# Decode of two layers on one core: both batches' values in one accumulator half, and three of eight value parts weighted on VectorE

## The chip, the cores and the metric

The kernel runs on 1 core of one Trainium2 chip. The metric is device time in microseconds (us), the median of several executions. Engines: PE (TensorE; PEld is its weight load), DVE (VectorE), ACT (ScalarE), POOL (GpSimd), SP (SyncE), whose queue issues nearly all the transfers here. A line such as L738 is a line of the kernel before.

## The reference

Two rounds of the same pair of blocks, on one new token of each of two batches: attention against a cache of 8192 keys and values, then a gated MLP. All in 32-bit floats.

```python
def _A_ref(x, k_cache, v_cache, wq, wo):          # x: 2 x 1 x 576, caches: 2 x 32 x 8192 x 128
    q = (x @ wq).reshape(2, 1, 32, 128).transpose(0, 2, 1, 3)
    scores = jnp.einsum("bhqd,bhkd->bhqk", q, k_cache) * (128 ** -0.5)
    p = _softmax(scores, axis=-1)
    o = jnp.einsum("bhqk,bhkd->bhqd", p, v_cache)
    return o.transpose(0, 2, 1, 3).reshape(2, 1, 32 * 128) @ wo

def _B_ref(x, w_gate, w_up, w_down):              # 576 -> 4608 -> 576
    return (_gelu(x @ w_gate) * (x @ w_up)) @ w_down

x = x + _A_ref(_layernorm(x), k_cache, v_cache, wq, wo)
x = x + _B_ref(_layernorm(x), w_gate, w_up, w_down)
x = x + _A_ref(_layernorm(x), k_cache, v_cache, wq, wo)
x = x + _B_ref(_layernorm(x), w_gate, w_up, w_down)
```

The caches are 268 MB each and both are read once in each round.

## The kernel before

**Items.** One round's attention is cut into 34 items. Items 0 to 29 are pairs: two neighbouring heads of one batch, 128 partitions by 128 rows of 128 floats, so 8.39 MB of keys and as much of values; batches alternate, so items 2k and 2k + 1 are the same two heads of batch 0 and of batch 1. Items 30 to 33 are single heads. The first layer goes through them from 0 to 33, the second from 33 to 0; a few keys and values at the turn are kept on the chip. An item has 8 parts (4 for a single head) of 16 rows each.

**Space.** `space` is one tile of SBUF in six slots; a pair of slots holds the keys or the values of one item, so three such buffers exist. `Arena` and `queue` plan the transfers when the program is built: a load is written into SP's queue as soon as the buffer it needs has been released by the code so far. In the steady part the values of item n go into the buffer that the keys of item n leave (released by the last reduction, L770), and the keys of a later item into the buffer that the values of item n leave (released by the matmul of the fold, L878). SP issues them in this order, keys and values in turn, and each waits for the instructions that release its buffer.

**Keys.** `multiply` (L738, DVE) multiplies keys with the query, which lies in PSUM (`bank`), in three units of 48, 48 and 32 rows; POOL adds the two halves of each row (L767); DVE adds up the 64 that are left (L770). `peak` and `highest` (L794 to L804) find the greatest score by way of a transpose on PE, `softmax` (L819, L827, ACT) writes the exponentials into `prz`, `total` and `inverse` (L835, L841) give the factor.

**Values.** `prz` holds the exponentials of an item with gaps of zeros, so that 8 neighbouring columns are the weights of a matmul: 4 rows of each of 2 heads. `values` (L899) runs one matmul for 4 rows of values, 128 x 512, into a band of 8 partitions of `acc`; the 4 groups of a part go to 4 bands. The pairs in the middle, 3 to 26, don't do this for all parts: `folds(n)` is true for them, and the last `FOLD` = 2 of 8 parts are weighted on DVE instead. `weigh` adds the exponentials of both heads into `share` (L865; one of them is zero), multiplies the values with them in place (L870), and lets POOL add halves onto each other until 4 rows are left (L873). `folded` (L878) brings these into `acc` by one more matmul, whose weights `owner` say which half of the partitions belongs to which head.

**Out of the accumulator.** `acc` has two halves of 512, and the pairs take them in turn. `gather` takes each item's own entries out of the bands: a product with `diag` (L913) and a sum (L914), on DVE. `context` turns the result by four matmuls (L921) into `po`, and `divide` (L940 on ACT) brings it into `oT`, from where `project` multiplies it with `wo`.

**Order.** The order on each engine is the order of the code, written out by hand (`tc.manual_schedule()`), one pass of the loop per item. In the pass of item n, with p the item before and a the one before that: `weigh(a)` comes first on DVE, ahead of the item's products; on POOL the adds of the fold stand ahead of the item's first L767; `softmax(p)` follows the first product; behind the second product come `total(p)`, `folded(a)`, `gather(a)`, `context(a)` and `values(p)`. Every engine takes its instructions in order.

```python
            if a is not None and folds(a):
                weigh(a)
            for j, (k, m) in enumerate(us):
                multiply(n, k, m)
```

Of the kernel before, what the change touches and what calls it, by code (L numbers as in the profile page):

```python
# [16 lines left out]
B = 2  # L17
# [28 lines left out]
FOLD = 2  # L46
# [78 lines left out]
def decode_layers(ctx, tc, x_in, kc, vc, wq, wo, wg, wu, wd, out):  # L125
# [32 lines left out]
    def part_at(at, n):  # L158
        return space[:, at:at + n]
# [285 lines left out]
    unit = consts.tile([P, 1], F32, name="unit")  # L445
    nc.vector.memset(unit, 1.0)
    ones = unit.to_broadcast([P, P])
    mhalf = consts.tile([P, 1], F32, name="mhalf")
    nc.vector.memset(mhalf, -0.5)

    pick = consts.tile([P, 4], F32, name="pick")
# [4 lines left out]
    diag = consts.tile([P, 4], F32, name="diag")  # L456
    of = consts.tile([P, B], F32, name="of")
    both = ident.rearrange("p (c v b r) -> p b r v c", c=4, v=4, b=B)[:, :, :, 0, :]
    scores = consts.tile([P, 2 * P], F32, name="scores")
    eight = scores[:, 0:4 * B].rearrange("p (b r) -> p b r", b=B)  # L460
    nc.vector.reduce_sum(eight, both, axis=AX.X)
    nc.vector.tensor_add(diag, eight[:, 0, :], eight[:, 1, :])
    nc.vector.reduce_sum(of, eight, axis=AX.X)
# [5 lines left out]
    sums = consts.tile([P, 2, 2], F32, name="sums")  # L469
    nc.vector.memset(sums, 0.0)  # L470

    side = consts.tile([P, 2], F32, name="side")
    nc.vector.reduce_sum(side, pick.rearrange("p (s b) -> p s b", s=2), axis=AX.X)

    owner = consts.tile([P, 2, 4], F32, name="owner")
    nc.vector.memset(owner, 0.0)
    for i in range(2):
        nc.vector.memset(owner[i * HALF:(i + 1) * HALF, i, :], 1.0)

    strip = consts.tile([P, 4], F32, name="strip")  # L480
# [11 lines left out]
    home = consts.tile([P, 3 * DH + 16], F32, name="home")  # L492
# [8 lines left out]
    for s in range(2):  # L501
# [8 lines left out]
    po = bank2[:, 0:2 * GH].rearrange("p (i c) -> p i c", c=2)  # L510
    turned = bank2[:, 2 * GH:2 * GH + P]
    smalls = [bank2[:, 2 * GH + P + 2 * i:2 * GH + P + 2 * i + 2] for i in range(2)]
    low = bank2[:, 2 * GH + P + 8:]
# [5 lines left out]
    rim, cut = two.shape[1] - 2 * DH, mid.shape[1]  # L519
    stash = [  # L520
        (2, rim, DH, low[:, :DH - rim], True),
        (3, 0, DH, low[:, DH - rim:2 * DH - rim], True),
        (4, 0, DH - rim, low[:, 2 * DH - rim:], True), (4, DH - rim, DH, two[:, 2 * DH:], False),
        (5, 0, cut, mid, True), (5, cut, DH, home[:, 3 * DH:], False),
# [77 lines left out]
    def attention(layer):  # L602
# [104 lines left out]
        def multiply(n, k, m):  # L707
# [7 lines left out]
            if n == SINGLE[1] and k == 0 and layer == 0:  # L715
                rest = ready[key_of(n)][2].rearrange("p j d -> p (j d)")[:, (JC - SPLIT[2]) * DH:]
                for to, lo in (
                    (spare, 0), (low, 2 * DH + rim), (qs[:, 2 * DH:], 5 * DH - rim), (mid, 5 * DH),
                    (home[:, 3 * DH:], 5 * DH + cut), (scores[:, DH // 2:DH // 2 + DH], 6 * DH),
# [473 lines left out]
```

## Time and profile before

| | before |
|---|---|
| time, median of 3 | 2683.82 us (2683.8 to 2685.11) |
| the profiled execution | 2683.47 us, span 2681.7 us |
| TensorE clock granted, mean | 0.629 |
| read from HBM | 1152.39 MB, 430 GB/s over the span |
| busy: PE, DVE, ACT, POOL | 912.3, 2027.3, 166.9, 1551.8 us |
| L738, products with the query (DVE) | 223, 1111.8 us |
| L767, adds of half rows (POOL) | 221, 1127.8 us |
| L770, reductions (DVE) | 223, 569.3 us |
| L899, matmuls on values (PE, two records each) | 3328, 509.6 us |
| L870, weighting of values (DVE) | 48, 212.2 us |
| L873, adds of the fold (POOL) | 144, 390.0 us |
| L913 and L914, gather (DVE) | 64 each, 43.5 and 44.2 us |

The span is from the first to the last instruction; the time also holds what lies around it. A row of the timeline has the start in us, the duration, engine, line, operation, what is written and read, shape and count, and in brackets how long the engine stood idle before and what ended that. A row of the groups has count, busy us and mean ns of one, then idle time before and its releasers. SPq is SP's queue: its rows are the issue of a transfer, not the transfer.

### The profile page before, as it was taken

What the parts mean: (1) busy time and instruction counts of PE and PEld (TensorE: products, weight loads), DVE (VectorE), ACT (ScalarE), POOL (GpSimd) and SP (SyncE); (2) the same over time, 40 slices, a digit from 0 to 9 for tenths busy, and PEclk for the clock granted to TensorE, in tenths of its full rate; (3) what the DMA queues carried; (4) which work ended last, traced back from release to release, by engine and by line L of the source; (5) the groups of instructions that cost most, each with busy time, mean ns of one, the idle gap of its engine ahead of it and who ended that gap; (6) DMA issues with size and microseconds to landing.
All of it is one profiled execution on the core that took longest, in us unless ns stands there. A gap on an engine that the chain in (4) does not pass through costs nothing. (4 is left out here: it accounts for less than half of the span.)

```text
span 2681.7 us, 16126 instructions
## 1 busy us (share of the span) xinstructions
PE 912.3 (34%) x6484; PEld 288.9 (11%) x6484; DVE 2027.3 (76%) x979; ACT 166.9 (6%) x797; POOL 1551.8 (58%) x408
## 2 busy tenths in 40 slices
PE   1323332233233233334663333223323323332346
PEld 0100010010001000111221101001000100010012
DVE  4878888888888888867037878888888888888740
ACT  0000000000000000000026000000000000000000
POOL 2546676667666766744028457666766666676520
PEclk8656655665566566566986665566566556655678
DMA  9999999999999999999999999999999999999998
GB/s 422 437 434 428 435 434 433 431 433 433 434 432 434 430 436 434 428 431 427 417 414 426 436 434 429 434 435 434 431 431 435 432 433 434 433 430 436 430 426 382
DMA packets 31498, 1153.44 MB, mean 430 GB/s; under 512 B 3880, under 2 KB 3904, under 8 KB 5696
## 3 DMA queue, kind: packets, MB, share of 16 engines
q1 hardware_dynamic: 31384, 1152.40, 99.8%
q8 instruction: 51, 0.84, 0.1%
q14 instruction: 23, 0.19, 0.0%
q10 hardware_dynamic: 40, 0.01, 0.0%
HBM read 1152.39 MB, written 0.00 MB: 430 GB/s over the span
## 5 line engine op out<-in xcount | busy, mean ns | idle before, releaser
L767 POOL TENSOR_TENSOR space<-space 128x3072 f32<-128x3072 f32 (+4 forms) x221 | 1127.8, 5103 | 474.8 <-DVE space L738 335.1
L738 DVE TENSOR_TENSOR space<-space,bank 128x6144 f32<-128x6144 f32 (+4 forms) x223 | 1111.8, 4987 | 300.4 <-DMA space<-in_A_k_cache_dram 230.6
L770 DVE TENSOR_REDUCE scores<-space 128x48 f32<-128x3072 f32 (+4 forms) x223 | 569.3, 2553 | 91.9 <-POOL space L767 91.7
L873 POOL TENSOR_TENSOR space<-space 128x2048 f32<-128x2048 f32 x144 | 390.0, 2708 | 385.7 <-DVE space L870 362.3
L899 PE MATMUL acc<-space,prz 128*8 128x512 f32 x3328 | 509.6, 776 | 206.6 <-DMA space<-in_A_v_cache_dram 202.5
L653 PE MATMUL bank<-qsb,pick 4*64 4x128 f32 (+1 forms) x256 | 45.4, 432 | 850.9 <-DVE space L738 843.3
L870 DVE TENSOR_TENSOR space<-space,bank 128x4096 f32<-128x4096 f32 x48 | 212.2, 4420 | 1.6
L899 PEld LDWEIGHTS acc<-space,prz 128*8 128x8 f32 x3328 | 98.7, 107 | 559.4 <-issue 356.8
L819 ACT ACTIVATE nbs<-bank 128x2 f32<-128x2 f32 (+1 forms) x68 | 11.6, 171 | 1812.4 <-PE bank L804 1782.8
L921 PE MATMUL bank<-of,wide 128*32 128x2 f32 x512 | 40.9, 202 | 237.9 <-DVE wide L914 237.9
L653 PEld LDWEIGHTS bank<-qsb,pick 4*64 4x64 f32 (+1 forms) x256 | 20.3, 200 | 872.3 <-DVE space L738 855.5
L796 PE MATMUL bank<-ident,m 128*1 128x128 f32 x68 | 21.7, 319 | 242.5 <-DVE m L794 242.3
L575 POOL TENSOR_TENSOR rstd<-ve,mhalf 128x1 f32<-128x1 f32 x4 | 2.2, 550 | 176.0 <-DVE ve L573 176.0
L878 PE MATMUL acc<-space,owner 128*8 128x512 f32 x96 | 89.9, 1039 | 0.0
L1124 DVE STREAM_TRANSPOSE gu<-acc 128x288 f32<-128x288 f32 x4 | 1.9, 483 | 93.2 <-ACT acc L1122 93.2
L921 PEld LDWEIGHTS bank<-of,wide 128*32 128x32 f32 x512 | 35.7, 154 | 326.1 <-DVE wide L914 324.9
L835 PE MATMUL bank<-sums,unit 128*128 128x2 f32 x120 | 35.2, 363 | 86.9 <-ACT prz L827 86.9
L913 DVE TENSOR_TENSOR acc<-acc,diag 128x512 f32<-128x512 f32 x64 | 43.5, 679 | 27.6 <-PE acc L899 27.6
L940 ACT ACTIVATE oT<-bank,rinv 32x8 f32<-32x8 f32 x110 | 28.5, 259 | 381.5 <-PE bank L921 380.8
L827 ACT ACTIVATE prz<-scores,nbs 64x128 f32<-64x128 f32 (+1 forms) x128 | 50.7, 396 | 17.2 <-POOL prz L817 14.4
L760 ACT ACTIVATE space<-space 128x128 f32<-128x128 f32 x164 | 48.4, 296 | 19.4 <-DVE space L738 16.5
L804 PE MATMUL bank<-m,unit 1*128 1x2 f32 (+1 forms) x136 | 38.5, 350 | 25.6 <-DVE m L802 25.6
(100 smaller groups left out, 519.0 us busy)
## 6 DMA issues: line engine op xcount, KB each, us to landing
space<-in_A_k_cache_dram SPq DMA_DIRECT2D x6, 4096.0 KB
space<-in_A_v_cache_dram SPq DMA_DIRECT2D x5, 4096.0 KB
space<-in_A_wo_dram SPq DMA_DIRECT2D x15, 1152.0 KB
space<-in_B_w_gate_dram SPq DMA_DIRECT2D x16, 576.0 KB
space<-in_B_w_up_dram SPq DMA_DIRECT2D x16, 576.0 KB
space<-in_B_w_down_dram SPq DMA_DIRECT2D x8, 1152.0 KB
space<-in_A_v_cache_dram SPq DMA_DIRECT2D x4, 2048.0 KB
space<-in_A_wq_dram SPq DMA_DIRECT2D x16, 512.0 KB
```

What stands on the lines that cost most here:

```text
L653: nc.tensor.matmul(qb[n][to, :], pick[32 * c:32 * c + 4, r:r + 1].to_broadcast([4, P // it.heads]), qsb[32 * c:32 * c + 4, (h % 4) * DH:(h ...
L738: nc.vector.tensor_tensor(out=u[:, :r, :], in0=t[:, :r, :], in1=qb[n].unsqueeze(1).to_broadcast([P, r, DH]), op=ALU.mult)
L760: nc.scalar.activation(u[:, j, :], u[:, j, :], AF.Copy, accum_out=S[n][:, base(n, k) + j:base(n, k) + j + 1])
L767: nc.gpsimd.tensor_tensor(out=half, in0=half, in1=u[:, :r, DH // 2:], op=ALU.add)
L770: nc.vector.tensor_reduce(out=S[n][:, base(n, k):base(n, k) + own_rows(n, k, m)], in_=prod.pop((n, k)), axis=AX.X, op=ALU.add)
L827: nc.scalar.activation(pr[at, lo:].rearrange("p (g e) -> p g e", e=4)[:, 0:it.rows // 2:2, :], s[at, :it.rows].rearrange("p (g r) -> p g r ...
L870: nc.vector.tensor_tensor(out=t, in0=t, in1=share.unsqueeze(2).to_broadcast([P, rows, DH]), op=ALU.mult)
L873: nc.gpsimd.tensor_tensor(out=t[:, :rows], in0=t[:, :rows], in1=t[:, rows:2 * rows], op=ALU.add)
L878: nc.tensor.matmul(accumulator(n)[0:8, :], owner.rearrange("p a e -> p (a e)"), part_at(arena.live[key, lo][0], 4 * DH), start=False, stop ...
L899: nc.tensor.matmul(accumulator(n)[32 * c:32 * c + 8, :], pr[:, at:at + 8], t[g // 4][:, g % 4 * 4:g % 4 * 4 + 4, :].rearrange("p j d -> p ...
L913: nc.vector.tensor_tensor(out=q, in0=q, in1=diag.unsqueeze(2).to_broadcast([P, 4, DH]), op=ALU.mult)
L921: nc.tensor.matmul(po[lo:lo + 32, i, :], t[:, i::GH], of, start=True, stop=True)
```

## The change

Three things are changed together.

1. The two items of the same heads share a half of `acc`. The bands get 16 partitions, 8 for each batch; a matmul on values has 16 columns of weights of which one batch's 8 are zeros. `prz` is one buffer for all pairs, with wider gaps. An item of batch 0 (in the first layer) begins a sum and the item of batch 1 completes it, so `gather`, `context` and `divide` are called once for two items, and `context` and `divide` write four columns instead of two. The constants (`diag`, `of`, `owner` and others) are laid out for this and moved into one tile, `few`.
2. `FOLD` is 3: three of eight parts are weighted and folded, five go to PE by `values`. The fold no longer halves alone: 48 rows become 24, 12, 8 and 4.
3. What was stored in `low` between the layers has less room there; a bit of it goes to a longer `home` (one more copy and one more product).

`weigh(f)` and `folded(f)` are called for every folded item, in the places where they were.

```diff
-FOLD = 2
+FOLD = 3
...
-    po = bank2[:, 0:2 * GH].rearrange("p (i c) -> p i c", c=2)
+    po = bank2[:, 0:4 * GH].rearrange("p (i c) -> p i c", c=4)
...
             if ITEMS[n].heads == 2:
-                return prz[:, 2 * (n % 2):2 * (n % 2) + 2, :].rearrange("p a e -> p (a e)")
+                return prz.rearrange("p a e -> p (a e)")
             return prz[:, n - PAIRS, :]
...
         def accumulator(n):
-            return acc[:, n % 2 if n < PAIRS else (n - PAIRS) // B, :]
+            return acc[:, (n // B + 1) % 2 if n < PAIRS else (n - PAIRS) // B, :]
 
         def completes(i):
 
-            return seq[i] < PAIRS or i > 0 and ITEMS[seq[i - 1]].h == ITEMS[seq[i]].h
+            return i > 0 and ITEMS[seq[i - 1]].h == ITEMS[seq[i]].h
...
             lo = ITEMS[n].parts - FOLD
-            pr = weights_of(n)[:, 2 * JC * lo:2 * JC * (lo + FOLD)].rearrange("p (g a e) -> p a g e", a=2, e=4)
+            pr = weights_of(n)[:, 8 + 4 * JC * lo:8 + 4 * JC * (lo + FOLD)].rearrange("p (g a e) -> p a g e", a=4, e=4)
...
             while rows > 4:
-                rows //= 2
-                nc.gpsimd.tensor_tensor(out=t[:, :rows], in0=t[:, :rows], in1=t[:, rows:2 * rows], op=ALU.add)
+                less = rows // 2 if rows % 8 == 0 else rows - 4
+                nc.gpsimd.tensor_tensor(
+                    out=t[:, :rows - less], in0=t[:, :rows - less], in1=t[:, less:rows], op=ALU.add
+                )
+                rows = less
...
             nc.tensor.matmul(
-                accumulator(n)[0:8, :], owner.rearrange("p a e -> p (a e)"), part_at(arena.live[key, lo][0], 4 * DH),
-                start=False, stop=True,
+                accumulator(n)[0:16, :], owner[:, 8 * ITEMS[n].b:8 * ITEMS[n].b + 16],
+                part_at(arena.live[key, lo][0], 4 * DH), start=False, stop=completes(seq.index(n)),
             )
...
-            begins = n < PAIRS or not completes(i)
+            begins = not completes(i)
...
-                at = 8 * g if it.heads == 2 else 8 * g + 4 - 4 * it.b
+                m = 8 * it.heads
+                at = m * g + m // 2 * (1 - it.b)
                 nc.tensor.matmul(
-                    accumulator(n)[32 * c:32 * c + 8, :], pr[:, at:at + 8],
+                    accumulator(n)[32 * c:32 * c + m, :], pr[:, at:at + m],
...
             a = seq[i - 2] if i > 1 and completes(i - 2) and not (layer == 0 and last) else None
+            f = seq[i - 2] if i > 1 and folds(seq[i - 2]) else None
...
-            if a is not None and folds(a):
-                weigh(a)
+            if f is not None:
+                weigh(f)
...
+                    if f is not None:
+                        folded(f)
                     if a is not None:
-                        if folds(a):
-                            folded(a)
                         gather(a)
```

How the instructions stand now, at three places in the middle of the first layer. First POOL, one item: the adds of the fold (L873, in the change L877) and of half rows (L767, L771). Before:

```order
L873 TENSOR_TENSOR space<-space 128x2048
L873 TENSOR_TENSOR space<-space 128x1024
L873 TENSOR_TENSOR space<-space 128x512
L767 TENSOR_TENSOR space<-space 128x48x64 x2
L767 TENSOR_TENSOR space<-space 128x32x64
```

and with the change:

```order
L877 TENSOR_TENSOR space<-space 128x3072
L877 TENSOR_TENSOR space<-space 128x1536
L877 TENSOR_TENSOR space<-space 128x512 x2
L771 TENSOR_TENSOR space<-space 128x48x64 x2
L771 TENSOR_TENSOR space<-space 128x32x64
```

The fold has four adds instead of three and still stands ahead of the item's first add of half rows.

Second DVE, one item from the weighting (L870, now L874) to the peak (L794, now L798). `space<-space,bank` are the products with the query, `scores<-space` the reductions, `acc<-acc` and `wide<-acc` the gather. Before:

```order
L870 TENSOR_TENSOR space<-space,bank_124 128x4096
L738 TENSOR_TENSOR space<-space,bank 128x6144
L802 TENSOR_REDUCE m_456<-bank_124 1x2
L738 TENSOR_TENSOR space<-space,bank 128x6144
L841 RECIPROCAL rinv<-bank_124 128x2
L913 TENSOR_TENSOR acc<-acc,diag 128x512
L914 TENSOR_REDUCE wide<-acc 128x128
L770 TENSOR_REDUCE scores<-space 128x48
L738 TENSOR_TENSOR space<-space,bank 128x4096
L770 TENSOR_REDUCE scores<-space 128x48
L770 TENSOR_REDUCE scores<-space 128x32
L794 TENSOR_REDUCE m<-scores 128x1
```

and with the change, an item without a gather:

```order
L874 TENSOR_TENSOR space<-space,bank_124 128x6144
L742 TENSOR_TENSOR space<-space,bank 128x6144
L806 TENSOR_REDUCE m_502<-bank_124 1x2
L742 TENSOR_TENSOR space<-space,bank 128x6144
L845 RECIPROCAL rinv<-bank_124 128x2
L774 TENSOR_REDUCE scores<-space 128x48
L742 TENSOR_TENSOR space<-space,bank 128x4096
L774 TENSOR_REDUCE scores<-space 128x48
L774 TENSOR_REDUCE scores<-space 128x32
L798 TENSOR_REDUCE m<-scores 128x1
```

The weighting is longer, in the same place; every second item lacks the gather (L921 and L922 in the others, behind L845 as before).

Third PE, from the sum of an item's exponentials (L835, now L839) by the fold's matmul (L878, now L885), the context (L921, now L930) and the matmuls on values (L899, now L907) to the transpose of the next peak. Before, one item:

```order
L835 MATMUL bank_124<-sums,unit 128x2
L878 MATMUL acc<-space,owner 8x512
L921 MATMUL bank_124<-of,wide 32x2 x4
L899 MATMUL acc<-space,prz 8x512 x24
L796 MATMUL bank_124<-ident,m 1x128
```

and with the change, two items:

```order
L839 MATMUL bank_124<-few 128x2
L885 MATMUL acc<-space,few 16x512
L930 MATMUL bank_124<-few,wide 32x4 x4
L907 MATMUL acc<-space,prz 16x512 x20
L800 MATMUL bank_124<-ident,m 1x128
L657 MATMUL bank<-qsb,few 64x128 x2
L808 MATMUL bank_124<-m_734,few 128x2
L839 MATMUL bank_124<-few 128x2
L885 MATMUL acc<-space,few 16x512
L907 MATMUL acc<-space,prz 16x512 x20
L800 MATMUL bank_124<-ident,m 1x128
```

The fold's matmul is there for both items, the context for one of two, and 20 matmuls on values are left of 24.

More of the change, by code (lines that the diff above doesn't have):

```diff
@@ L814, in softmax @@
             nb, s, pr = mT.pop(n), S.pop(n), weights_of(n)
[L816 removed]
+            if n in (SINGLE if layer == 0 else (PAIRS - 1,)):
                 nc.gpsimd.memset(pr, 0.0)
@@ L1046, in attention @@
         inverse(n)
-        finish(seq[-3] if layer == 0 else p)
+        if layer == 0:
+            finish(seq[-3])
         if layer == 0:
```

70 lines of the change are left out of this document (37 added, 33 removed).

## The prediction

> **What bounds the kernel now.** I read the page's totals first, then busy time by stage, then one item in order of time, then the groups by line.
>
> ```profile
> span 2681.7 us, 16126 instructions
> ...
> q1 hardware_dynamic: 31384, 1152.40, 99.8%
> ```
> ```profile
> core 0: us, PE busy (x) PEld busy (x) DVE busy (x) ACT busy (x) POOL busy (x), PEclk, DMA share, GB/s
> 1649.41:2502.95 853.54, 264.49 (x1474) 75.03 (x1474) 719.54 (x286) 36.78 (x154) 573.06 (x133) 0.59 1.00 433
> 2600.00:2682.00 82.00, 45.38 (x656) 19.00 (x656) 5.88 (x22) 1.77 (x6) 0.55 (x1) 0.78 0.92 391
> ```
>
> One DMA queue carries everything and its engines are busy 99.8% of the span. The first window is the steady part of the second layer: DMA share 1.00 at 433 GB/s, so no time can be won there by making an engine's work shorter. The last window has the one visible gap, and the change does not touch that stage. The question is therefore only whether the engines, after the change, still keep ahead of the stream. The start and the end of that window are the same instruction, 22 items apart, in the chain of waits:
>
> ```profile
> 1649.41 6.56 DVE space L738
> ...
> 2502.95 6.57 DVE space L738
> ```
>
> So the stream gives one item (8.39 MB of keys, 8.39 MB of values) every 853.54/22 = 38.80 us. Now one item in the timeline, on DVE, POOL, PE and SP's queue:
>
> ```profile
> 1927.24 6.69 POOL L767 TENSOR_TENSOR space<-space 128x3072 f32<-128x3072 f32 x1 [1.59 <-issue]
> ...
> 1934.45 0.68 DVE L913 TENSOR_TENSOR acc<-acc,diag 128x512 f32<-128x512 f32 x1
> ...
> 1935.16 0.69 DVE L914 TENSOR_REDUCE wide<-acc 128x128 f32<-128x512 f32 x1
> 1935.77 3.34 DVE L770 TENSOR_REDUCE scores<-space 128x48 f32<-128x3072 f32 x1
> ...
> 1939.03 4.41 DVE L738 TENSOR_TENSOR space<-space,bank 128x4096 f32<-128x4096 f32 x1
> ...
> 1939.92 8.26 PE L899 MATMUL acc<-space,prz 128*8 128x512 f32 x48 [3.38 <-DMA space<-in_A_v_cache_dram]
> ...
> 1943.58 4.55 POOL L767 TENSOR_TENSOR space<-space 128x2048 f32<-128x2048 f32 x1 [2.37 <-DVE space L738]
> ...
> 1948.16 2.29 DVE L770 TENSOR_REDUCE scores<-space 128x32 f32<-128x2048 f32 x1 [1.46 <-POOL space L767]
> 1950.48 0.33 SPq L167 DMA_DIRECT2D space<-in_A_v_cache_dram  x1
> ...
> 1951.22 0.20 DVE L865 TENSOR_TENSOR bank<-prz 128x32 f32<-128x32 f32 x1 [0.45 <-PE bank L796]
> 1951.46 4.42 DVE L870 TENSOR_TENSOR space<-space,bank 128x4096 f32<-128x4096 f32 x1
> 1955.96 8.28 POOL L873 TENSOR_TENSOR space<-space 128x2048 f32<-128x2048 f32 x3 [7.83 <-DVE space L870]
> 1959.34 6.55 DVE L738 TENSOR_TENSOR space<-space,bank 128x6144 f32<-128x6144 f32 x1 [3.46 <-DMA space<-in_A_k_cache_dram]
> ...
> 1966.03 6.70 POOL L767 TENSOR_TENSOR space<-space 128x3072 f32<-128x3072 f32 x1 [1.79 <-issue]
> ...
> 1968.96 1.87 PE L878 MATMUL acc<-space,owner 128*8 128x512 f32 x2
> 1970.86 0.33 SPq L167 DMA_DIRECT2D space<-in_A_k_cache_dram  x1
> ```
>
> Read it as a ring over DVE and POOL. From POOL's first add of an item (L767): the reduction waits for it, 6.69 + 0.03 (the hand-over seen at 1943.58 + 4.55 = 1948.13 against 1948.16); reduction to third product 1939.03 - 1935.77 = 3.26; third product to third add 4.55; that add to its reduction 4.58; that reduction to L870 3.30; L870 to the fold 4.50; the fold 8.28; and then about 0.10 until POOL, which takes its queue in order, can start the next item's first add. Sum 35.29 us, against 38.80 us of the stream. The margin is 3.5 us, and it is visible: DVE stands idle 3.46 us for the keys at 1959.34, and POOL 1.79 us after the fold.
>
> SP's lead is the other number. The value load is issued at 1950.48 while the keys before it land at 1959.34: 8.86 us ahead. The key load at 1970.86 waits for the fold's matmul.
>
> **The change part by part.** The prices of the forms:
>
> ```profile
> L767 POOL TENSOR_TENSOR space<-space 128x3072 f32<-128x3072 f32 x114 | 762.9, 6692 | 253.6 <-DVE space L738 132.2 <-issue 79.5 <-DVE rinv L841 32.6
> ...
> L873 POOL TENSOR_TENSOR space<-space 128x2048 f32<-128x2048 f32 x48 | 216.0, 4500 | 378.2 <-DVE space L870 362.3 <-issue 15.9
> ...
> L873 POOL TENSOR_TENSOR space<-space 128x1024 f32<-128x1024 f32 x48 | 113.1, 2356 | 3.8
> L873 POOL TENSOR_TENSOR space<-space 128x512 f32<-128x512 f32 x48 | 60.9, 1269 | 3.8
> ```
>
> *Weighting.* L870 grows from 4096 to 6144 elements. L738 costs the same at 4096 (4.41 and 4.42), so L738's 6.55 for 6144 (1959.34): +2.13 us an item. The sum ahead of it (L865) goes from 32 to 48 elements: +0.02.
>
> *Fold.* Three adds (2048, 1024, 512) become four: 3072, 1536, 512, 512. The first costs 6.69 by the L767 row; extending L873's own line (1024 more elements cost 2.14) gives 6.64; I take the former. 1536 lies between 2.36 and 4.50; the three rows lie on a line (2.12 and 2.09 ns an element), so 3.43. Twice 1.27. The gaps are (8.28 - 4.50 - 2.36 - 1.27)/2 = 0.08 each, three of them. Together 12.90 us: +4.62.
>
> *What they displace.* Both stand on the ring, in series, since the fold waits for the whole weighting and POOL's next add waits behind the fold. New ring: 35.29 + 2.13 + 0.02 + 4.62 = 42.06 us, 3.26 more than the stream. The 3.5 us of margin is used up, and from then on the stream waits for slots. SP's lead covers this once.
>
> *Gathers.* 30 of the 64 pairs of L913 and L914 go. One takes 1935.77 - 1934.45 = 1.32 us. On DVE it stands ahead of the first reduction; with POOL late, that reduction waits for POOL's add anyway: matmul 1.87 + gather 1.32 + hand-overs 0.2 end about 3.4 us after the add has begun, which itself takes 6.69. So the saving is worth nothing, and the gathers that stay cost nothing; without that cover the 12 left in the folded items of each layer would cost 2 x 12 x 1.32 = 32 us.
>
> *PE and ACT.* 20 value matmuls instead of 24, context and divide once for two batches: both engines are idle most of an item (264.49 us busy of 853.54 on PE). Nothing. Wider weights (16 columns for 8) have no row; the same 512 columns stream past, so I take nothing, and a doubled fold matmul (+1.87) would still lie beside the 6.69.
>
> *One weight buffer for all pairs.* The exponentials of an item must now wait until the item before has been weighted and multiplied. DVE weights before it finds the next item's peak, and the value matmuls (8.26 us from 1939.92) end 17 us before the L738 at 1959.34, behind which that peak is known. Nothing; if the matmuls were that late, they would hold PE's queue and with it the peak.
>
> *The stored rows.* One more short copy on ACT and one more short product between the layers, under 0.5 us each, beside a running stream.
>
> **The sum.** Of 24 folded items in each layer (48 in all, the count of the fold's rows) the first does not run on the ring yet. Its predecessor has no gather now, so L870 starts 24.22 - 1.32 = 22.90 us after POOL's first add (1951.46 - 1927.24); + 6.63 + 0.02 + 12.90 + 0.10 = 42.55, less 38.80: late by 3.75. Each of the 23 others adds 3.26: 75.0. Lateness at the end of a layer's folds 78.7 us. From it goes SP's lead: 8.86, and 1.8 because on the ring the value load follows POOL's first add by 21.4 us (6.72 + 3.26 + 4.55 + 4.58 + 2.32) instead of 23.24; less what a transfer needs to begin, which no row gives. Its bounds are nothing and the whole of a small one:
>
> ```profile
> 2678.72 0.65 SPq L1165 DMA_DIRECT2D out_dram<-x  x1
> ```
>
> It ends by the span's end, 3.0 us later. I take 1.5 (between, both include more or less than a start). Lead 9.2, so each layer loses 69.5 us of stream, both 139. The unfolded items catch up with the stream but the stream cannot regain its idle time. The profiled execution took 2683.47 us (0.35 below the median of 2683.82): 2683.5 + 139 = **2822 us**.
>
> **Rivals.** (1) *The ring still closes under the stream*, so the loads stay ahead: the fold would have to cost at most 12.90 - 3.26 + 0.38 = 10.0 us (0.38 = 9.2/24, the lead spread out), that is 1.78 ns for each of 5632 elements. For it speaks only that POOL's long forms might be relatively cheaper; against it, 3072 elements cost 2.18 ns each and 2048 cost 2.20. Time: the stream's, 2683 us, give or take 6 (a stream at 432 or 434 instead of 433 GB/s). Not slower.
>
> (2) *POOL takes longer than its bars show.* From the fold's start to POOL's next start are 10.07 us (1955.96 to 1966.03), not 8.28. Scaled by 1.216 the new fold costs 15.69, the ring 44.85; a layer loses 6.5 + 23 x 6.05 - 9.2 = 136.5, the time is 2957. Against it: the reduction starts 0.03 after the bar of POOL's third add ends, so a bar's end is a real end; and POOL's start at 1966.03 follows the end of L738 at 1965.89. The Trainium skill ("Perfetto Trace Analysis", section "GPSIMD Engine Instruction") says to time such instructions by the spacing of their starts and not by the reported span. By that rule the sum would be this rival's; the two hand-overs above disagree with it here.
>
> **How the numbers follow.** Forecast 88%, rival 1 7%, rival 2 5%. The forecast's own spread: the ring is 42.06 give or take 0.5 (the 1536 form, gaps, hand-overs), times 46 is 23 us; the lead between 7.7 and 10.7 a layer, 3 us. That is 2796 to 2848. I reach a little further toward rival 1, to 2785, and to 2850 above; rival 2 and most of rival 1 stay outside. What a measurement tells from no change is 0.2%, 5 us: slower 93%, the same 4%, faster 3% (rival 1's edges).
>
> **What would show it.** Right: first products (L742 there) of folded items about 42 us apart instead of 38.8; DVE's wait for keys nearly gone, its wait for POOL at the first reduction 3 to 6 us an item; POOL without a gap between fold and first add; DMA share about 0.92 and some 400 GB/s in the folded stretches, unchanged elsewhere; a fold near 12.9 us. Wrong: DVE still waiting for keys in every item, or DMA share at 1.00 there (rival 1); a fold well over 13 us from start to next start (rival 2). If the spacing is 42 but the loss clearly less than 130, the lead was misjudged.

## The result, and the profile after

The changed kernel took 2819.22 us (median of four runs, 2818.9 to 2820.43) beside 2683.81 us of the kernel before (2683.33 to 2685.11): 135.4 us more, a ratio of 1.0505 with a 95% interval of 1.0489 to 1.052. The forecast was 2822 us, in a range of 2785 to 2850. Lines are those of the changed kernel now, 4 to 9 higher than in the kernel before: L742 is L738, L771 is L767, L774 is L770, L874 is L870, L877 is L873, L885 is L878, L921 is L913, L922 is L914.

Two rows of the page of the changed kernel: the busy time of each engine, and the queue that carries the caches with its packets, MB and share of the span.

```profile
PE 841.7 (30%) x5860; PEld 290.7 (10%) x5860; DVE 2095.9 (74%) x930; ACT 166.6 (6%) x796; POOL 1765.6 (63%) x455
...
q1 hardware_dynamic: 31384, 1152.40, 96.1%
```

PE works 71 us less than in the table before, DVE and POOL 69 and 214 us more, and the queue is busy 96.1% instead of 99.8%: the same bytes, with idle time in between. Where the idle time lies, shows busy time by stage, here three stretches of the changed kernel (length, then busy us and instructions of each engine, the granted clock, DMA share, GB/s):

```profile
0.00:160.00 160.00, 36.22 (x245) 11.33 (x245) 103.18 (x67) 6.62 (x22) 65.12 (x18) 0.70 1.00 430
...
350.00:1200.00 850.00, 216.72 (x1126) 73.18 (x1128) 692.06 (x242) 34.62 (x145) 621.33 (x145) 0.58 0.94 399
...
1700.00:2600.00 900.00, 229.95 (x1190) 75.09 (x1180) 736.52 (x259) 34.62 (x145) 648.94 (x150) 0.58 0.95 402
```

Ahead of the folded items, whose first fold starts at 217.61, the queue is full (share 1.00, 430 GB/s). In the folded stretches of both layers it has 0.94 and 0.95, at 399 and 402 GB/s (0.92 and some 400 were forecast). One item there, by the timeline of the changed kernel (start, us, engine, line; in brackets the idle time before and what ended it):

```profile
2012.55 12.91 POOL L877 TENSOR_TENSOR space<-space 128x3072 f32<-128x3072 f32 x4 [10.06 <-DVE space L874]
...
2025.42 13.37 POOL L771 TENSOR_TENSOR space<-space 128x3072 f32<-128x3072 f32 x2
...
2025.52 1.89 PE L885 MATMUL acc<-space,few 128*16 128x512 f32 x2 [3.46 <-POOL space L877]
...
2027.43 0.33 SPq L167 DMA_DIRECT2D space<-in_A_k_cache_dram  x1
2027.44 0.70 DVE L921 TENSOR_TENSOR acc<-acc,few 128x512 f32<-128x512 f32 x1 [1.08 <-PE acc L885]
...
2032.14 3.35 DVE L774 TENSOR_REDUCE scores<-space 128x48 f32<-128x3072 f32 x1 [3.27 <-POOL space L771]
...
2035.41 4.41 DVE L742 TENSOR_TENSOR space<-space,bank 128x4096 f32<-128x4096 f32 x1
...
2039.90 4.50 POOL L771 TENSOR_TENSOR space<-space 128x2048 f32<-128x2048 f32 x1 [1.11 <-DVE space L742]
2044.44 2.29 DVE L774 TENSOR_REDUCE scores<-space 128x32 f32<-128x2048 f32 x1 [1.35 <-POOL space L771]
2046.75 0.33 SPq L167 DMA_DIRECT2D space<-in_A_v_cache_dram  x1
...
2047.85 6.55 DVE L874 TENSOR_TENSOR space<-space,bank 128x6144 f32<-128x6144 f32 x1
...
2054.49 12.92 POOL L877 TENSOR_TENSOR space<-space 128x3072 f32<-128x3072 f32 x4 [10.08 <-DVE space L874]
...
2067.36 6.70 POOL L771 TENSOR_TENSOR space<-space 128x3072 f32<-128x3072 f32 x1
```

This is the ring of the prediction with its waits. None of its instructions waits for a load (the two issues of SP, the matmul L885 and the gather's L921 are shown beside it), and it comes round in 2067.36 - 2025.42 = 41.94 us. The chain of waits of the changed kernel (start, us, engine, buffer, line) agrees over a whole layer. Between these two rows, 22 items apart, it consists of DVE and POOL, but for the transpose of each item's peak on PE (L800, some 0.4 us between the last reduction and the weighting):

```profile
230.50 13.30 POOL space L771 x2
...
1153.17 13.33 POOL space L771 x2
```

(1153.17 - 230.50)/22 = 41.94 us. The stream's 38.80 us are no longer what an item takes. Two rows of each kernel's list of DVE's waits (what waits for what: us in all, times, longest) show who now waits for whom. Before:

```profile
DVE space L738 <- DMA space<-in_A_k_cache_dram: 230.6, 57, 16.6
...
DVE scores L770 <- POOL space L767: 91.7, 64, 2.6
```

and after:

```profile
DVE scores L774 <- POOL space L771: 300.8, 112, 5.8
...
DVE space L742 <- DMA space<-in_A_k_cache_dram: 64.5, 11, 16.6
```

The wait for keys has shrunk from 57 times to 11; the wait for POOL's adds stands in its place. At an item's first reduction it is 3.27 us where DVE has a gather to do, and 5.8 us where it has none: the gather only fills time that DVE would wait.

### The profile page after: what moved, and what is told of

It is laid out like the page before. It is cut to its first block, busy times and chain, and to the rows that moved or that the text cites. A ratio compares the mean times of both kernels' runs of the same rounds, so it can differ in the third digit from the quotient of the medians.

```text
span 2818.6 us, 14794 instructions
## 1 busy us (share of the span) xinstructions
PE 841.7 (30%) x5860; PEld 290.7 (10%) x5860; DVE 2095.9 (74%) x930; ACT 166.6 (6%) x796; POOL 1765.6 (63%) x455
## 3 DMA queue, kind: packets, MB, share of 16 engines
q1 hardware_dynamic: 31384, 1152.40, 96.1%
## 4 chain that ended last, share of the span: by engine, by line
POOL 53%; DVE 22%; DMA 12%; issue 3%; PE 2%; ACT 1%; SPq 0%; POOLq 0%; DVEq 0%; ACTq 0%
POOL space L771 31%; POOL space L877 22%; DVE space L874 11%; DVE scores L774 5%; DMA space<-in_A_k_cache_dram 4%; DVE space L742 4%; DMA space<-in_B_w_up_dram 3%; DMA space<-in_B_w_down_dram 2%; DMA space<-in_A_v_cache_dram 2%; DMA space<-in_A_wo_dram 1%; PE bank L800 1%; DVE m L798 1%; ACT space L764 0%; DVE bank L869 0%; DMA space<-in_B_w_gate_dram 0%
## 5 line engine op out<-in xcount | busy, mean ns | idle before, releaser
L771 POOL TENSOR_TENSOR space<-space 128x3072 f32<-128x3072 f32 (+4 forms) x221 | 1124.9, 5100 | 289.4 <-DVE space L742 271.6
L742 DVE TENSOR_TENSOR space<-space,bank 128x6144 f32<-128x6144 f32 (+4 forms) x223 | 1111.6, 4986 | 135.9 <-DMA space<-in_A_k_cache_dram 64.5
L877 POOL TENSOR_TENSOR space<-space 128x3072 f32<-128x3072 f32 x192 | 608.9, 3171 | 494.6 <-DVE space L874 473.3
L774 DVE TENSOR_REDUCE scores<-space 128x48 f32<-128x3072 f32 (+4 forms) x223 | 569.8, 2555 | 301.0 <-POOL space L771 300.8
L907 PE MATMUL acc<-space,prz 128*16 128x512 f32 (+1 forms) x2944 | 461.1, 784 | 105.3 <-DMA space<-in_A_v_cache_dram 101.2
L874 DVE TENSOR_TENSOR space<-space,bank 128x6144 f32<-128x6144 f32 x48 | 314.6, 6554 | 1.6
L657 PE MATMUL bank<-qsb,few 4*64 4x128 f32 (+1 forms) x256 | 45.7, 434 | 789.2 <-DVE space L742 781.6
L800 PE MATMUL bank<-ident,m 128*1 128x128 f32 x68 | 24.3, 357 | 635.4 <-DVE m L798 635.3
L907 PEld LDWEIGHTS acc<-space,prz 128*16 128x16 f32 (+1 forms) x2944 | 120.4, 117 | 424.0 <-issue 294.1
L885 PE MATMUL acc<-space,few 128*16 128x512 f32 x96 | 90.6, 1047 | 160.8 <-POOL space L877 160.8
L800 PEld LDWEIGHTS bank<-ident,m 128*1 128x1 f32 x68 | 5.4, 79 | 691.3 <-DVE m L798 380.0
L921 DVE TENSOR_TENSOR acc<-acc,few 128x512 f32<-128x512 f32 x34 | 23.6, 694 | 52.9 <-PE acc L907 28.9
L839 PE MATMUL bank<-few 128*128 128x2 f32 x120 | 35.1, 362 | 81.4 <-ACT prz L831 81.4
L808 PE MATMUL bank<-m,few 1*128 1x2 f32 (+1 forms) x136 | 38.8, 352 | 19.5 <-DVE m L806 19.5
L930 PE MATMUL bank<-few,wide 128*32 128x4 f32 (+1 forms) x272 | 21.8, 203 | 66.2 <-DVE wide L922 66.2
```

The lines of the kernel that those rows point to most:

```text
L657: nc.tensor.matmul(qb[n][to, :], pick[32 * c:32 * c + 4, r:r + 1].to_broadcast([4, P // it.heads]), qsb[32 * c:32 * c + 4, (h % 4) * DH:(h ...
L742: nc.vector.tensor_tensor(out=u[:, :r, :], in0=t[:, :r, :], in1=qb[n].unsqueeze(1).to_broadcast([P, r, DH]), op=ALU.mult)
L771: nc.gpsimd.tensor_tensor(out=half, in0=half, in1=u[:, :r, DH // 2:], op=ALU.add)
L774: nc.vector.tensor_reduce(out=S[n][:, base(n, k):base(n, k) + own_rows(n, k, m)], in_=prod.pop((n, k)), axis=AX.X, op=ALU.add)
L800: nc.tensor.transpose(mT[n], m, ident)
L808: nc.tensor.matmul(mT[n][:, :heads], ones[0:1, :], m1[:, :heads], start=True, stop=True)
```

## The experiments

The theory is the ring: an item's time is the greater of the stream's 38.80 us and of the sum of hand-overs round DVE and POOL; what goes beyond counts once for each of 24 folded items of a layer, less a lead of SP that is paid out once a layer. Its rivals: that the shared accumulator half and its waits cost the time; that POOL's work slows the transfers in proportion, by contention, with no threshold; and that POOL's adds matter alone, not what stands on the ring beside them.

| run | edit | us (median) | ratio, 95% interval |
|---|---|---|---|
| e1_share_only | the change with FOLD 2 | 2683.67 | 0.9992 to 1.001 |
| e2_fold3_only | before with FOLD 3 | 2823.22 | 1.0506 to 1.0534 |
| e3_pool_1024 | before + POOL add, 1024 | 2683.32 | 0.999 to 1.0009 |
| e4_pool_2048 | before + POOL add, 2048 | 2683.73 | 0.9989 to 1.0009 |
| e5_pool_3072 | before + POOL add, 3072 | 2750.65 | 1.0235 to 1.0265 |
| e9_dve_memsets | before + DVE memsets | 2714.04 | 1.01 to 1.013 |
| e8_fold1 | before with FOLD 1 | 2684.12 | 0.9994 to 1.0012 |
| e6_six_matmuls | the change, fold's short adds on PE | 2770.86 | 1.0304 to 1.0337 |
| e11_repeat_matmul | before, fold's matmul six times | 2754.03 | 1.0234 to 1.0269 |
| e10_three_matmuls | the change, last two adds on PE | 2702.18 | 1.0054 to 1.0084 |
| e7_fold_behind_add | the change, fold behind the first add | 3267.55 | 1.2127 to 1.2232 |

**Which part of the change.** Each half alone: first the changed kernel with the old share of folding.

```diff
-FOLD = 3
+FOLD = 2
```

> The change with FOLD = 2: both batches share an accumulator half, half of the gathers are gone, one weight buffer, 16 columns of weights, but two parts are weighted and folded as before. Ring theory (DVE and POOL in series, L870, fold, next first add): 35.3 us an item, under the stream's 38.8, so 2683.8 us within 3, DMA share 1.00, DVE still waiting 3 us or more for keys in the items of the middle. Rival 'sharing' (wider weights, one weight buffer or the longer accumulation hold the slots): about 2819 us. Rival 'contention' (the stream loses in proportion to what POOL does, 135 us for 214 us more POOL time): 2684.

Measured 2683.67 us. The stage by busy time, 22 items of this run:

```profile
1649.41:2502.95 853.54, 256.42 (x1386) 72.08 (x1386) 705.68 (x265) 36.77 (x154) 572.28 (x132) 0.59 1.00 433
```

Share 1.00 and 433 GB/s, as before the change. And the kernel before with the longer fold, and with the changed fold's loop, since 48 rows don't halve to 4:

```diff
-FOLD = 2
+FOLD = 3
...
-                rows //= 2
-                nc.gpsimd.tensor_tensor(out=t[:, :rows], in0=t[:, :rows], in1=t[:, rows:2 * rows], op=ALU.add)
+                less = rows // 2 if rows % 8 == 0 else rows - 4
+                nc.gpsimd.tensor_tensor(
+                    out=t[:, :rows - less], in0=t[:, :rows - less], in1=t[:, less:rows], op=ALU.add
+                )
+                rows = less
```

> The kernel before with three parts weighted and folded (48, 24, 12, 8, 4 rows), nothing shared, all 64 gathers left. Ring theory: 42.0 us an item as in the changed kernel; the gathers lie beside POOL's first add and cost nothing, only the first folded item is 1.3 us later, so 2819 to 2825 us. Rival 'sharing': 2684. Rival 'contention': 2819. If the gathers did lie on the ring, 1.32 us more an item against the changed kernel's 0.66: 2850.

Measured 2823.22 us, with a ring of the same length (timeline of this run, POOL's first adds of two items, between them the gather's second half and the first reduction):

```profile
2028.13 13.37 POOL L767 TENSOR_TENSOR space<-space 128x3072 f32<-128x3072 f32 x2
...
2030.87 0.69 DVE L917 TENSOR_REDUCE wide<-acc 128x128 f32<-128x512 f32 x1
...
2034.84 3.35 DVE L770 TENSOR_REDUCE scores<-space 128x48 f32<-128x3072 f32 x1 [3.28 <-POOL space L767]
...
2070.06 6.69 POOL L767 TENSOR_TENSOR space<-space 128x3072 f32<-128x3072 f32 x1
```

2070.06 - 2028.13 = 41.93 us. So the third part is the whole loss, and sharing the accumulator costs nothing; with three parts it saves the 4 us between this run and the changed kernel. The gathers, which this run has in every item, are over at 2031.56, 3.28 us before the reduction can start: they lie under POOL's add, as the prediction had it. Of the 4 us, 2 x 1.35 come from the way in: the interval of the first folded item is 43.79 us here and 42.44 there, about the 1.32 us of a gather, once in each layer. The rest, some 1.4 us, goes with the lead, further down.

**Is it POOL's time on the ring, and is there a threshold?** The kernel before, with one more add on POOL behind the fold, on rows that nothing reads any more; 8, 16 or 24 rows of 128 elements:

```diff
+            spent = t[:, 8:8 + 8]
+            nc.gpsimd.tensor_tensor(out=spent, in0=spent, in1=spent, op=ALU.add)
```

> The kernel before with one more POOL add of 1024 elements behind each fold, on rows that nothing reads any more (2.36 + 0.08 us on the ring). Ring theory: 35.3 + 2.4 = 37.7 us, still under 38.8: 2684 within 3. Rival 'contention' (0.63 us for each us of POOL time): +72, 2756.

> The same with an add of 2048 elements (4.50 + 0.08). Ring theory: 39.87 us, 1.07 more than the stream; a layer is late by 2.9 + 23 x 1.07 = 27.5, less a lead of 8.2 (the changed kernel's loss of 67.7 a layer against its lateness of 75.9): 19 a layer, 2722 us (2705 to 2740). Rival 'contention': +137, 2821.

> The same with an add of 3072 elements (6.69 + 0.08). Ring theory: 42.06 us, as in the changed kernel though DVE does no more than before: 2819 to 2825 us. Rival 'sharing': 2684. Rival 'contention': +203, 2887.

Measured 2683.32, 2683.73 and 2750.65 us. The second and third miss, and the groups by form say why (count, busy us, mean ns of one). Of the run with 2048:

```profile
L875 POOL TENSOR_TENSOR space<-space 128x2048 f32<-128x2048 f32 x48 | 172.8, 3600 | 0.0
```

and with 3072:

```profile
L875 POOL TENSOR_TENSOR space<-space 128x3072 f32<-128x3072 f32 x48 | 254.6, 5304 | 0.0
```

An add whose two inputs and output are the same rows is cheaper than the fold's (5304 ns instead of 6692). With the measured prices the theory stands: 35.29 + 3.60 = 38.89 us is as good as the stream's 38.80, and nothing is lost; 35.29 + 5.30 is 40.59, and the timeline of the run with 3072 shows (first add, the keys' issue, next first add)

```profile
2020.00 13.37 POOL L767 TENSOR_TENSOR space<-space 128x3072 f32<-128x3072 f32 x2
2020.06 0.33 SPq L167 DMA_DIRECT2D space<-in_A_k_cache_dram  x1
...
2060.50 6.66 POOL L767 TENSOR_TENSOR space<-space 128x3072 f32<-128x3072 f32 x1
```

40.50 us from first add to first add. Between 3.60 and 5.30 us of POOL's work an item the time begins to rise, and 48 x 3.60 = 173 us of added work cost nothing. Contention in proportion to POOL's work would have shown at 1024 and 2048; it is refuted.

**Is it the ring, or POOL?** Two memsets on DVE ahead of the weighting, and POOL as before:

```diff
+            for _ in range(2):
+                nc.vector.memset(kept, 0.0)
```

> The kernel before with two memsets of 128 x 2048 on DVE ahead of each weighting, of a PSUM tile that is not in use then (about 2.0 to 2.2 us each by the 0.485 us of 512 elements); POOL's work as before. Ring theory: DVE's time there counts like POOL's: 35.3 + 4.2 = 39.5 us, 2700 to 2725 us. If only POOL's time counted: 2684. Rival 'contention': 2684.

Measured 2714.04 us. In the timeline of this run (POOL's first add and the issue of the keys):

```profile
2030.40 13.39 POOL L767 TENSOR_TENSOR space<-space 128x3072 f32<-128x3072 f32 x2
...
2033.47 0.33 SPq L167 DMA_DIRECT2D space<-in_A_k_cache_dram  x1
...
2069.97 6.70 POOL L767 TENSOR_TENSOR space<-space 128x3072 f32<-128x3072 f32 x1
```

39.57 us: with 4.28 us more between L865 and the weighting (4.52 instead of 0.24), 35.29 + 4.28. It is the ring, whichever of the two engines it grows on. The opposite direction, one part folded instead of two:

```diff
-FOLD = 2
+FOLD = 1
```

> The kernel before with one part weighted and folded (16, 8, 4 rows). Ring theory: the ring is about 28.5 us, far under 38.8, and a wider margin is worth nothing: 2683.8 within 3, DVE's wait for keys 10 us an item. PE takes 28 value matmuls instead of 24, 1.4 us more, hidden. Rival 'contention': faster, POOL does 210 us less.

Measured 2684.12 us. The stream sets the pace, and the shorter weighting became a longer wait of DVE for keys (335.5 us in this run's list of waits, 230.6 before). That wait was expected at 10 us an item and is 5.4 to 6.4: DVE gains the 2.13 us of its own weighting, while POOL's saving turns into idle time on POOL (8.59 us behind one fold, 1.79 before).

**Can the fold be had more cheaply?** In place of POOL's adds of 24, 12 and 8 rows, six matmuls of 4 rows each, in the same sum:

```diff
-            while rows > 4:
+            while rows > 24:
...
+            for k in range(6):
+                nc.tensor.matmul(
+                    accumulator(n)[0:16, :], owner[:, 8 * ITEMS[n].b:8 * ITEMS[n].b + 16],
+                    part_at(arena.live[key, lo][0] + 4 * DH * k, 4 * DH), start=False,
+                    stop=completes(seq.index(n)) and k == 5,
+                )
```

> The changed kernel, three parts weighted, but POOL folds only once (48 rows to 24, 6.7 us instead of 12.9) and PE takes the 24 rows in six matmuls instead of one. Ring theory: 41.94 - 6.2 = 35.7 us an item, under the stream: 2684 us within 3, though DVE still does 2.13 us more weighting an item than before. Rival 'sharing': about 2819. Rival 'contention' (POOL's fold 322 us in all against 390 before): at or below 2684. If PE's ten further matmul records an item on the way to the key load cost a lead of 8 us: 4 to 5 us later issue, still hidden.

Measured 2770.86 us: a third of the loss is back, not all of it. The timeline of this run, two items from first product (L742) to first product, with the fold's matmuls (L886), the gather (L923), the issues of keys and the values' matmuls (L909):

```profile
2056.69 6.55 DVE L742 TENSOR_TENSOR space<-space,bank 128x6144 f32<-128x6144 f32 x1 [2.82 <-DMA space<-in_A_k_cache_dram]
...
2066.31 8.16 PE L886 MATMUL acc<-space,few 128*16 128x512 f32 x12
...
2074.50 0.70 DVE L923 TENSOR_TENSOR acc<-acc,few 128x512 f32<-128x512 f32 x1 [3.83 <-PE acc L886]
2074.53 0.33 SPq L167 DMA_DIRECT2D space<-in_A_k_cache_dram  x1
...
2098.28 6.55 DVE L742 TENSOR_TENSOR space<-space,bank 128x6144 f32<-128x6144 f32 x1
...
2115.81 0.33 SPq L167 DMA_DIRECT2D space<-in_A_k_cache_dram  x1
...
2117.68 4.48 PE L909 MATMUL acc<-space,prz 128*16 128x512 f32 x40 [1.94 <-DMA space<-in_A_v_cache_dram]
...
2140.27 6.55 DVE L742 TENSOR_TENSOR space<-space,bank 128x6144 f32<-128x6144 f32 x1 [5.77 <-DMA space<-in_A_k_cache_dram]
```

POOL's part of the fold is down to its first add, and the ring through POOL is short enough: POOL stands idle 2.70 us before the item's first add. But twelve records on PE take 8.16 us, behind that add and the sum, and two things wait for their end. The gather waits 3.83 us, and with it DVE's first reduction, which POOL's first add (2063.38, 6.71 us) would have let go at 2070.1: this item takes 2098.28 - 2056.69 = 41.59 us, with DVE waiting for keys no more than 0.2 us at its end. And the next keys are issued 2074.53 - 2056.69 = 17.8 us after the keys before were there, where the kernel before had 1970.86 - 1959.34 = 11.5. In the next item, which has no gather, that load is late: issued at 2115.81, 1.87 us before the values ahead of it are there (2117.68), its keys are there at 2140.27, 22.59 us behind the values, where half of the stream's item is 19.40, and DVE waits 5.77 us for them. So there is a second loop, through PE.

The items are not as even as on the ring: the intervals between first products lie between 38.9 and 42.3 us, 40.7 in the mean.

To see whether PE's matmuls alone do it, the kernel before with its one matmul six times over:

```diff
+            for k in range(6):
+                nc.tensor.matmul(
+                    accumulator(n)[0:8, :], owner.rearrange("p a e -> p (a e)"),
+                    part_at(arena.live[key, lo][0], 4 * DH), start=False, stop=k == 5,
+                )
```

> The kernel before with the matmul of each fold done six times (the folded rows come into the sum six times over, so the result is another). DVE's and POOL's work is that of the kernel before. If the loss of the kernel with six matmuls lies in PE's way to the key load: ten more records of 0.63 us make the key load 6.3 us later, 17.8 us after the keys before landed, some 1.6 us ahead of the values' landing (19.4); the transfer then lands 24.5 us after its issue as seen there, so the keys come every 41 to 42 us instead of 38.8, and the gather, here in every item, waits 3 to 4 us for PE: 2750 to 2820 us. If the loss there was the 2.13 us of weighting on DVE: 2684. Ring of DVE and POOL alone: 2684.

Measured 2754.03 us (2745.76 to 2762.69; the trace is of the slowest), at the lower end of what was expected, with POOL's and DVE's work untouched. Its timeline, in an item that is shorter than most:

```profile
2016.58 6.55 DVE L738 TENSOR_TENSOR space<-space,bank 128x6144 f32<-128x6144 f32 x1 [2.79 <-DMA space<-in_A_k_cache_dram]
...
2026.19 7.60 PE L879 MATMUL acc<-space,owner 128*8 128x512 f32 x12
...
2033.83 0.70 DVE L914 TENSOR_TENSOR acc<-acc,diag 128x512 f32<-128x512 f32 x1 [3.27 <-PE acc L879]
2033.87 0.33 SPq L167 DMA_DIRECT2D space<-in_A_k_cache_dram  x1
...
2055.67 6.55 DVE L738 TENSOR_TENSOR space<-space,bank 128x6144 f32<-128x6144 f32 x1 [0.33 <-DMA space<-in_A_k_cache_dram]
```

They do: the gather waits 3.27 us, the keys are issued 17.3 us after the keys before were there, and the item takes 39.09 us, with DVE waiting for keys at its end. The next item takes 41.11 us: its keys are issued at 2072.20, 16.5 us after the keys before were there, and are there at 2096.78, with DVE waiting 3.09 us. The intervals lie between 38.7 and 42.4 us, 40.5 in the mean; 46 times the excess of 1.7 us is 78 us, about the whole loss of this trace.

Both waits come from one instruction, and no run takes them apart; but the traces show which of them ends last. In this run each of the 48 folded items ends with DVE waiting for keys (0.28 to 3.39 us), so the load sets the time, not the gather. In the run with six matmuls the items without a gather end so (2.6 to 5.8 us), and most of those with one don't: there it is the gather. So three matmuls, with the adds of 24 and 12 rows left to POOL:

```diff
-            while rows > 4:
+            while rows > 12:
...
+            for k in range(3):
```

> The changed kernel with POOL folding 48 rows to 24 and 12, and PE taking the 12 rows in three matmuls. Ring theory: 41.94 - 2.7 = 39.25 us, 0.45 more than the stream; late by 1 + 23 x 0.45 = 11.4 a layer, less a lead of 8.2: 2690 us (2684 to 2705). PE: four more records, 2.6 us, so the key load comes 4.5 us after POOL's first add begins as before the change (4.8); it should cost nothing. If PE's part costs as in the kernel with six matmuls, in proportion 0.4 of 87 us on top: 2725.

Measured 2702.18 us. Its timeline, first add, issue of the keys, next first add:

```profile
2020.85 13.36 POOL L771 TENSOR_TENSOR space<-space 128x3072 f32<-128x3072 f32 x2
...
2025.84 0.33 SPq L167 DMA_DIRECT2D space<-in_A_k_cache_dram  x1
...
2060.12 6.69 POOL L771 TENSOR_TENSOR space<-space 128x3072 f32<-128x3072 f32 x1
```

2060.12 - 2020.85 = 39.27 us (expected 39.25), but more was lost than that ring alone explains with the changed kernel's lead; see below.

**Where the fold stands.** The changed kernel with POOL's adds of the fold behind the next item's first add, so that the first reduction doesn't wait for them:

```diff
+            return t, rows
+
+        def fold(t, rows):
...
-                weigh(f)
+                weighed = weigh(f)
...
                 multiply(n, k, m)
+                if j == 0 and f is not None:
+                    fold(*weighed)
```

> The changed kernel with POOL's fold behind the item's first add of half rows instead of ahead of it; same instructions on every engine. Ring theory: the fold then delays the second and third add, and its matmul and the key load behind it; the ring from POOL's first add is fold end 19.7 + matmul 2.0 + transfer start 1.5 + transfer 19.4 + product 6.6 = about 49 us, through the key load: near 3170 us (3100 to 3200), slower than the changed kernel. Without the transfer on it, 47.5 us and 3070. If what costs is that the first add waits for the fold, taking that wait away gives 2684 to 2750. Rival 'contention' or engine time: 2819 as before the move.

Measured 3267.55 us: the direction was right and the size 100 us short. The timeline of this run: the issue of keys, the first product that waits for them, that item's first add, its gather, and the next item's first add.

```profile
1983.22 0.33 SPq L167 DMA_DIRECT2D space<-in_A_k_cache_dram  x1
...
2005.02 6.55 DVE L742 TENSOR_TENSOR space<-space,bank 128x6144 f32<-128x6144 f32 x1 [2.65 <-DMA space<-in_A_k_cache_dram]
...
2011.71 6.70 POOL L771 TENSOR_TENSOR space<-space 128x3072 f32<-128x3072 f32 x1 [19.32 <-DVE space L742]
...
2033.16 0.70 DVE L925 TENSOR_TENSOR acc<-acc,few 128x512 f32<-128x512 f32 x1 [14.16 <-PE acc L889]
...
2063.36 6.70 POOL L771 TENSOR_TENSOR space<-space 128x3072 f32<-128x3072 f32 x1 [16.60 <-DVE space L742]
```

Two kinds of items take turns. The one without a gather, whose first add began at 1961.73, takes 2011.71 - 1961.73 = 49.98 us, and it is the ring through the key load that was expected at 49 us: the keys are issued behind the fold's matmul, they are there 2005.02 - 1983.22 = 21.80 us later (20.9 were reckoned), and DVE waits 2.65 us for them. The item with a gather takes 2063.36 - 2011.71 = 51.65 us, without a wait for keys: its gather waits 14.16 us for the fold's matmul, and everything else of DVE waits behind it in its queue. So the fold's matmul holds up both; the cover that the prediction gave the gathers is gone, but that makes only some 1.6 us between the two kinds.

No run of the eleven is faster than the kernel before beyond what can be told apart; those in which the ring and the matmuls keep ahead (e1, e3, e4, e8) are all at 2683.3 to 2684.1 us, the stream's time.

## Why the prediction was right

**The bound.** It held that the stream sets the pace before, that nothing can be won there, and that 3.5 us of margin decide. e1 and e8 confirm the first half, e3 to e5 and e9 the margin.

**The prices.** Two groups by form of the changed kernel (count, busy us, mean ns):

```profile
L877 POOL TENSOR_TENSOR space<-space 128x3072 f32<-128x3072 f32 x48 | 321.7, 6702 | 483.3 <-DVE space L874 473.3 <-issue 10.0
...
L877 POOL TENSOR_TENSOR space<-space 128x1536 f32<-128x1536 f32 x48 | 165.2, 3442 | 3.8
```

Predicted 6.69 and 3.43 us; measured 6.702 and 3.442. The weighting, predicted at 6.55, took 6.55 in the timeline above. The fold's bar in the timeline is 12.91 or 12.92 for 12.90.

**The ring, piece by piece**, by the timeline of the changed kernel above:

| from, to | predicted | measured |
|---|---|---|
| first add, first reduction | 6.72 | 6.72 |
| to third product | 3.26 | 3.27 |
| to third add | 4.55 | 4.49 |
| to its reduction | 4.58 | 4.54 |
| to the weighting | 3.32 | 3.41 |
| to the fold | 6.63 | 6.64 |
| to the next first add | 13.00 | 12.87 |
| sum | 42.06 | 41.94 |

The 0.10 us between fold and first add that were carried over from before are gone: the first add's product is long done, and POOL goes on at once.

**The gathers, PE, ACT, one weight buffer.** Priced at nothing, and so they are: the gather's L921 waits 1.08 us for its matmul, and it and L922 (0.69 us) are done when the reduction is still waiting 3.27 us for POOL; e1 has all of these edits but the 20 value matmuls, and with the stream setting the pace neither its 30 gathers fewer gain anything nor do its new waits cost anything. The fold's matmul with 16 columns took 1.89 us in the timeline, 1.87 with 8.

**The sum.** The first folded item was late by 42.44 - 38.80 = 3.64 us (predicted 3.75), 23 others by 3.14 (3.26): 75.9 us a layer. Each layer lost 135.4/2 = 67.7. So the lead was worth 8.2 us, predicted 9.2; it is what is left over, not measured by itself, so that this sum closes by construction. The three differences, 2 x 23 x 0.12 = 5.5 and 2 x 0.1 us less, 2 x 1.0 more, make the 139 of the forecast into 135.3. The ring, a little too long, and the lead, a little too large, were off in opposite directions, so the total came out nearer than the ring alone would have put it.

**The lead is the weak term.** It was reckoned as one number for a layer, from the issue of the values. The runs show that it isn't one:

| run | ring, us | late a layer | lost a layer | lead | keys' issue after first add |
|---|---|---|---|---|---|
| e5_pool_3072 | 40.50 | 42.7 | 33.5 | 9.2 | 0.06 |
| the change | 41.94 | 75.9 | 67.7 | 8.2 | 2.0 |
| e2_fold3_only | 41.94 | 77.2 | 69.9 | 7.3 | 2.0 |
| e9_dve_memsets | 39.57 | 20.3 | 15.2 | 5.1 | 3.1 |
| e10_three_matmuls | 39.25 | 12.3 | 9.3 | 3.0 | 4.2 to 6.5 |

Late is the sum of what the intervals between first adds of the 24 folded items of the first layer exceed 38.80 us by; lost is half of the whole loss; the lead is the difference. The values are issued 21.3 to 21.6 us after the first add in all of them (but for the ends of a layer). What falls with the lead is the place of the other load, the keys, whose release is the fold's matmul. The prediction left that out: it counted only the value load. The traces show at which of the two loads the stream stops. In the changed kernel no transfer is recorded from 2025.50 to 2028.00 (DMA share 0.00), where the keys are issued; from 2046.00 to 2048.50, where the values are, the share is 1.04. The spacing of the issues says the same: 19.32 us from keys to values, no more than a load takes, but 22.62 from values to the next keys (2069.37 - 2046.75). In e2, e9 and e10 it is so too (18.4 and 21.2 us in e9). Only in e5 are the values the late ones (21.32 from keys to values, 19.18 to the next keys), and only there was the lead the 9.2 us of the forecast. So the prediction reckoned the lead at the value load, while the changed kernel loses its time at the key load; that its 9.2 is only 1 us from the 8.2 left over was luck. Besides, the 1.5 us that a transfer was given to begin were too few: the keys of e7 took 21.80 us into an idle queue, 2.40 more than the stream's 19.40. That the key's place causes the difference is seen in five runs, not tried by itself, and it is not the whole account: the changed kernel and e2 issue the keys at the same place, with leads of 8.2 and 7.3.

**The rivals.** The ring didn't close under the stream (rival 1): the fold costs what its forms cost. POOL doesn't take longer than its bars (rival 2): from the fold's start at 2012.55 to POOL's next start at 2025.42 are 12.87 us, and the bar is 12.91. Scaled, it would have been 15.69. The 10.07 us of the kernel before were a wait for DVE's product. By the rule of the Trainium skill ("Perfetto Trace Analysis", section "GPSIMD Engine Instruction"), to time such instructions by the spacing of their starts, the fold now costs the same as by its bar; rule and bar agree here, where POOL doesn't wait in between.

## What to carry to other kernels

In a kernel that streams from memory, add up the hand-overs once round the loop of engines that work in order, and compare the sum with the stream's time for an item; busy shares of 58 and 76% didn't show that POOL and DVE together had 3.5 us of 38.80 left. In these runs work on that loop was free up to its margin, and then cost the whole excess in every item, on whichever engine it stood; taking work off a loop that had a margin already brought nothing (e8). A cure for one loop must also be followed along the others, to the instruction that releases the next buffer above all: moving 2.7 to 6.2 us of the fold from POOL to PE shortened the loop through POOL and delayed the load and the gather.

## What was not expected of the hardware

- POOL's add depends on its operands: with both inputs and the output on the same rows, 1892, 3600 and 5304 ns for 1024, 2048 and 3072 elements (1.73 to 1.85 ns an element); with two different inputs 4500 ns for 2048 and 6692 for 3072 (2.18 to 2.20).
- A load into an idle queue took longer than one in the stream: in e7 the keys were there 21.80 us after their issue, and in e6 one issued 1.87 us before its predecessor was there came 22.59 us behind it, where loads in the unbroken stream follow each other by 19.40.
- The fold's matmuls in e6 (128 x 512, 16 columns of weights) took 8.16/12 = 0.68 us a record in a row in the item shown (0.65 in the next), against 1.89/2 = 0.94 for a single one; the granted clock over the run was 0.677 with them and 0.623 without.
